# Scores of a banded attention in four 64x64 quarters of TensorE, with the two triangles merged per half block

## The chip, the cores and the metric

One core of one Trainium2 chip. The metric is the device time of one execution in microseconds, taken as the median of several runs. TensorE is called PE below, its weight loads PEld, VectorE DVE, ScalarE ACT, GpSimd POOL, and the queue of SyncE, which issues the transfers, SP.

## The reference

Attention over a band of 128 keys, with a linear bias, and a gated FFN on its output, all in fp32:

```python
B, H, S, D = 8, 8, 576, 64
scores = q @ k.T / sqrt(D)                      # per batch and head
rel = pos[:, None] - pos[None, :]
scores = where((rel >= 0) & (rel < 128), scores - slope[h] * abs(rel), -1e9)
attn = exp(scores - max); attn = attn / (sum(attn) + 1e-9)
x = (attn @ v), heads put side by side          # 4608 tokens x 512
out = (sigmoid(x @ w_gate) * (x @ w_val)) @ w_out   # 512 -> 1536 -> 512
```

## The kernel before

**Attention.** Two heads of a batch make a unit (32 units). Their 2 x 576 tokens are laid end to end and cut into 9 blocks of 128 queries, so that block 4 holds the end of one head and the start of the other. A block i needs the keys of blocks i-1 and i: in the band of 128, query row r sees key column c of its own block where c <= r, and key column c of the block before where c > r. So of the 256 scores of a row just 128 count, one in each column c, and the kernel merges the two triangles into one 128 x 128 tile.

The head size of 64 fills half of the rows of the array. The keys lie twice in SBUF, on partitions 0 to 63 and 64 to 127, and the queries of even and odd blocks on the one half or the other (`kraw`, `qraw`). The 288 blocks of all units form one stream. `scores` (L332) takes a call of 8 of them at a time, or of 4 for the first 72 blocks: block k of the call runs on row half r = k % 2 and is number a = k // 2 there. L346 multiplies 128 queries (weights) by 256 keys (128 for i = 0, which has no block before it) into half of a PSUM bank. There are four such banks, `sp` = mm2 to mm5, two for each row half; a bank holds two blocks. An fp32 matmul runs as two passes, each with its own weight load and its own row in the profile.

Then follow, in this order:

- L359, DVE: one copy_predicated per bank copies, where the mask `before` (L203, key column > row) is set, the score of the block before over that of the own block, for both blocks of the bank at once
- L367, DVE: per block, bias added, scaled, and the minimum (the negated maximum) of each row taken, from PSUM to the SBUF tile `pb`
- L370, ACT: exp, with the sum of each row
- L385, L387, DVE, for three blocks at once: 1 / sum; L390 on ACT or L391 on DVE: the product with it
- L395, PE: three blocks transposed; L178 on ACT (or L179 on DVE): copied to SBUF; L406, POOL: split into the two triangles again
- L432, PE: the value call, one per unit. It uses the array as two column halves of 64, one for each head of the unit, all 128 rows each, 13 matmuls with two passes. Its loop (L418 to L427) gives the columns that stream: for the first head 3 x 256 + 128 + 64 + 64 = 1024, for the second 192 + 256 + 256 + 192 + 64 + 64 + 64 = 1088.

**FFN.** A first pass over four of the twelve chunks of the hidden size (L474 gate and value, L513 output) runs beside the attention, on PE in every gap of it. Its weights are decoded early on ACT and DVE (L265 to L269, then L178, L179 and L187). A second pass over the other chunks (L605 and L513) follows.

**Order.** All operations go into one graph with a cost, a time at which they are wanted (`want`) and, for the attention, an earliest time (`release`). `Graph.order` simulates the engines with these costs and always picks the operation that can start first, among equals the one wanted first; FFN matmuls are wanted last. The result is the order in which each engine gets its instructions: engines work in that order and wait on semaphores. In the first 30 us `warm` (L232) fills gaps that the planner sees on PE with matmuls on the identity.

Of the kernel before, what the change touches and what calls it, by code (L numbers as in the profile page):

```python
# [9 lines left out]
I32 = mybir.dt.int32  # L10
F32R = mybir.dt.float32r
AF = mybir.ActivationFunctionType
ALU = mybir.AluOpType
PSUM = bass.MemoryType.PSUM

P = 128
B, H, S, D = 8, 8, 576, 64
# [14 lines left out]
RUN = 8  # L32
# [115 lines left out]
def dve_cost(n, psum=False, two=False):  # L148
    return 0.07 + n * (0.00104 if psum or two else 0.00053)
# [7 lines left out]
def attention_gated_ffn(ctx: ExitStack, tc: tile.TileContext, qd, kd, vd, wg, wv, wo, out):  # L157
    nc = tc.nc
    ctx.enter_context(tc.manual_schedule())
    g = Graph()  # L160
# [6 lines left out]
    att = att_ctx.enter_context(tc.tile_pool(name="att", bufs=1))  # L167
# [3 lines left out]
    def T(pool, name, shape, dtype, tag=None):  # L171
        if name not in made:
            made[name] = pool.tile(shape, dtype, tag=tag or name, name=name)
        return made[name]
# [22 lines left out]

    rel = moe.tile([P, 3, P], F32, tag="pi0", name="rel")
    nc.gpsimd.iota(rel[:, 0], [[-1, P]], base=0, channel_multiplier=1, allow_small_or_imprecise_dtypes=True)
    before = att.tile([P, 2, P], I32, name="before")  # L200
    nc.vector.tensor_scalar(rel[:, 1], rel[:, 0], 0.0, None, op0=ALU.is_lt)
    for a in range(2):
        nc.vector.tensor_copy(before[:, a], rel[:, 1])  # L203
    nc.vector.scalar_tensor_tensor(rel[:, 2], rel[:, 1], float(P), rel[:, 0], op0=ALU.mult, op1=ALU.add)
    relm = [att.tile([P, 5, P], F32, name=f"relm{p}") for p in range(NPAIR)]
    f = -8.0 * 2.0 ** -1
# [18 lines left out]
    mm = [ps_m.tile([P, NB], F32, name=f"mm{i}") for i in range(8)]  # L225
    sp = [t.rearrange("p (a q) -> p a q", a=2) for t in mm[2:6]]
# [80 lines left out]
    kraw = lambda u: T(att, f"kr{u.l}", [P, TOK], F32)  # L307
    qraw = lambda u: T(att, f"qr{u.l}", [P, (NBLK + 1) // 2, P], F32)
# [16 lines left out]
    def three_of(u, i):  # L325
        m = u.n * TRI + i // TRI
        e = i % TRI
        st = lambda: T(att, f"st{m % NST}", [P, 9], F32)
        pb = lambda: T(att, f"pb{m % NPB}", [P, TRI, P], F32)
        return m, e, st, pb, ("st", m % NST), ("pb", m % NPB)  # L330

    def scores(blks):  # L332

        u0, i0 = blks[0]
        want = u0.when(i0)
        slack = 0.0 if u0.n < HEAD else SLACK
        spot = [(k % 2, k // 2) for k in range(len(blks))]
        half = len(blks) == RUN // 2 and stages[0] % 2
        stages[0] += 1
        bank_of = lambda r, a: r * (RUN // 4) + a // 2 + half  # L340

        def matmuls():
            for (u, i), (r, a) in zip(blks, spot):
                lo = P if i == 0 else 0
                rows = slice(r * D, r * D + D)
                nc.tensor.matmul(sp[bank_of(r, a)][:, a % 2, lo:], qraw(u)[rows, i // 2],  # L346
                                 kraw(u)[rows, (i - 1) * P + lo:(i + 1) * P], start=True, stop=True)

        used = {}
        for (u, i), (r, a) in zip(blks, spot):  # L350
            used.setdefault(bank_of(r, a), []).append((u, i, a % 2))
        cost = sum(max(0.216 if i == 0 else 0.432 for (u, i), (r, b) in zip(blks, spot) if b == a) for a in {a for r, a in spot})
        g.add("PE", cost, matmuls, [("qr", u.l, i) for u, i in blks] + [("kr", u.l, j) for u, i in blks for j in (i - 1, i) if j >= 0],
              [("mm", 2 + b) for b in used], want, slack=slack, release=max(u.rel(i) for u, i in blks), mode=1)
        for b, on in sorted(used.items(), key=lambda kv: blks.index(kv[1][0][:2])):
            a = [a for u, i, a in on if i]
            if a:
                a0, a1 = a[0], a[-1] + 1
                g.add("DVE", dve_cost((a1 - a0) * P, psum=True), lambda b=b, a0=a0, a1=a1: nc.vector.copy_predicated(  # L359
                    sp[b][:, a0:a1, P:], before[:, a0:a1], sp[b][:, a0:a1, 0:P]), ["before"], [("mm", 2 + b)], want)  # L360
        for (u, i), (r, a) in zip(blks, spot):
            def one(u, i, b, a):
                m, e, st, pb, kst, kpb = three_of(u, i)
                want = u.when(i)
                mid = NBLK // 2
                w = 0 if i == 0 else 1 if i < mid else min(4, i - mid + 2)
                g.add("DVE", 0.21, lambda: nc.vector.tensor_tensor_reduce(  # L367
                    pb()[:, e], sp[b][:, a, P:], relm[u.p][:, w], op0=ALU.add, op1=ALU.min,
                    scale=-0.125, scalar=3.0e38, accum_out=st()[:, e:e + 1]), [("mm", 2 + b)], [(kpb, e), (kst, e)], want)
                g.add("ACT", 0.39, lambda: nc.scalar.activation(  # L370
                    pb()[:, e], pb()[:, e], AF.Exp, bias=st()[:, e:e + 1], scale=-1.0, accum_out=st()[:, 3 + e:4 + e]),
                    [(kst, e)], [(kpb, e), (kst, 3 + e)], want)
            one(u, i, bank_of(r, a), a % 2)
            if i % TRI == TRI - 1:
                probabilities(u, i - TRI + 1)
            if i == NBLK - 1:
                values(u)
# [282 lines left out]
    for u in units:  # L660
        if u.n + NSLOT - 1 < len(units):
            load(units[u.n + NSLOT - 1])
        while at < (u.n + 1) * NBLK:
            n = RUN // 2 if at < SOON * NBLK else RUN
            scores(stream[at:at + n])
            at += n
        if u.n == 0:
            todo = [(src, kind, i) for i0 in range(0, FC1, GRP) for src, kind in ((wg, "g"), (wv, "v")) for i in range(i0, i0 + GRP)]
            for k, (src, kind, i) in enumerate(todo + [(wo, "o", i) for i in range(FC1)]):
                prepare(w1, src, kind, i, W0 + WSTEP * k)  # L670
        if u.p == NPAIR - 1:
            while todo1 and (todo1[0] + 1) * NB <= (u.b + 1) * S:
                if todo1[0] >= LATE and banks[0] == 2:
                    banks[0] = 8
                    g.add("PY", 0.0, lambda: None, [], [TP, TAIL], FIRST)
                ffn(todo1.pop(0), w1)
# [11 lines left out]
    for f0 in range(FC1, NFC, FC1):  # L688
        w = Weights("w2", lambda: pools["w2"], list(range(f0, f0 + FC1)), ["w2pool"])
# [68 lines left out]
```

## Time and profile before

| | |
|---|---|
| median of 3 runs | 1048.82 us (1048.61 to 1049.87) |
| profiled execution: span, first to last instruction | 1047.7 us |
| busy: PE, PEld | 1036.2, 905.9 us |
| busy: DVE, ACT, POOL | 702.9, 518.1, 109.4 us |
| L346, scores on PE | 576 passes, 74.2 us |
| L359, merges on DVE | 144 |
| L432, values on PE | 832 passes, 67.4 us |

For the profiled execution the page gives the span; its time with what lies around the span is not listed, so sums are made against the span or, with the difference of 1.1 us left as it is, against the median.

In the groups, `64*128 64x256` is a weight tile of 64 rows by 128 columns and 64 partitions by 256 elements of the moving operand. A number after the bar is the time in which at least one instruction of the group ran, and after the comma the mean length of one in ns; instructions of one engine overlap, so count times mean can exceed the busy time. In a timeline, a row starts at its first number and lasts for its second. In rows of windows, the number in brackets counts instructions.

### The profile page before, as it was taken

The page shows a single profiled execution, that of the slowest core. Times are in us where ns is not written, and L with a number is a line of the kernel's source. Part 1 is how long each engine was busy: PE and PEld are TensorE (multiplying, and loading weights), DVE is VectorE, ACT ScalarE, POOL GpSimd, SP SyncE. Part 2 cuts the span into 40 slices and gives each one's busy share as a digit, 9 for nine tenths or more (in the row PEclk, how much of TensorE's full clock was granted, in tenths as well). Part 3 has the DMA queues.
Part 4 walks back from the last instruction along what each step waited for, and adds up shares of the span by engine and source line. Part 5 has one row for each costly group of instructions (what it writes and reads, how often), then busy time and mean ns, then how long its engine had stood idle before and what let it go on. Part 6 is the DMA issues. An engine that isn't in the chain of part 4 may idle for free.

```text
span 1047.7 us, 17053 instructions
## 1 busy us (share of the span) xinstructions
PE 1036.2 (99%) x5952; PEld 905.9 (86%) x5952; DVE 702.9 (67%) x1989; ACT 518.1 (49%) x1421; POOL 109.4 (10%) x202
## 2 busy tenths in 40 slices
PE   9999999999999999999999999999999999999998
PEld 7677777888887888888989999898999989899997
DVE  8989857565756249855757465666998566574643
ACT  6998757566755534432425243352744335242331
POOL 2423222222222210000000000000010000000000
PEclk9999999999999999999999999999999999999999
DMA  8767654554551315540241523324362241505112
GB/s 290 249 219 247 227 169 157 160 188 123 173 197 46 115 61 180 183 162 31 91 152 31 181 71 110 115 67 156 106 228 97 98 141 42 171 16 176 65 57 101
DMA packets 74726, 142.67 MB, mean 136 GB/s; under 512 B 7312, under 2 KB 30224, under 8 KB 74640
## 3 DMA queue, kind: packets, MB, share of 16 engines
q1 hardware_dynamic: 74640, 141.58, 41.1%
q8 instruction: 47, 0.77, 0.3%
q14 instruction: 39, 0.32, 0.1%
HBM read 103.81 MB, written 37.75 MB: 135 GB/s over the span
## 4 chain that ended last, share of the span: by engine, by line
PE 93%; DVE 3%; ACT 3%; DMA 0%; issue 0%; SPq 0%; ACTq 0%; DVEq 0%
PE mm L605 33%; PE mm L513 28%; PE mm L474 18%; PE mm L346 5%; PE mm L432 5%; PE mm L395 3%; ACT pb L370 1%; DVE wbits L269 1%; DVE mm L359 0%; DVE pb L367 0%; DMA kr<-in_k_dram 0%; PE mm L232 0%; ACT both L178 0%; ACT pb L390 0%; DVE pb L391 0%
## 5 line engine op out<-in xcount | busy, mean ns | idle before, releaser
L605 PE MATMUL mm<-xc,w2s 128*128 128x384 f32 x2016 | 354.4, 335 | 0.0
L605 PEld LDWEIGHTS mm<-xc,w2s 128*128 128x128 f32 x2016 | 351.3, 188 | 2.0
L513 PE MATMUL mm<-w2o,hh 128*128 128x512 f32 x576 | 177.7, 390 | 0.0
L406 POOL TENSOR_SCALAR_AFFINE_SELECT pt<-both 128x384 f32<-128x384 f32 x192 | 103.8, 564 | 268.9 <-ACT both L178 257.2
L513 PEld LDWEIGHTS mm<-w2o,hh 128*128 128x128 f32 x576 | 107.8, 188 | 21.2
L370 ACT ACTIVATE pb<-pb,st 128x128 f32<-128x128 f32 x288 | 112.7, 395 | 26.0 <-DVE st L367 25.8
L513 PE MATMUL mm<-w2o,hl 128*128 128x512 f32 x288 | 112.4, 390 | 0.0
L616 ACT ACTIVATE sg<-mm 128x384 f32<-128x384 f32 x96 | 47.2, 493 | 116.7 <-PE mm L605 77.7
L178 ACT COPY a<-mm 128x384 f32<-128x384 f32 x48 | 23.1, 482 | 151.8 <-PE mm L605 148.8
L513 PE MATMUL mm<-w1o,hh 128*128 128x512 f32 x288 | 92.2, 401 | 1.2 <-DVE hl L187 1.2
L474 PE MATMUL mm<-xhi,w1v 128*128 128x512 f32 x288 | 91.8, 400 | 1.0 <-ACT sg L485 1.0
L474 PE MATMUL mm<-xhi,w1g 128*128 128x512 f32 x288 | 92.4, 402 | 0.0
L612 DVE TENSOR_TENSOR mm<-mm,a 128x384 f32<-128x384 f32 x48 | 27.1, 564 | 74.7 <-PE mm L605 74.7
L359 DVE COPY_PREDICATED mm<-before,mm 128x256 f32<-128x256 int32 (+1 forms) x144 | 50.3, 394 | 37.3 <-PE mm L346 36.3
L346 PE MATMUL mm<-kr,qr 64*128 64x256 f32 (+1 forms) x576 | 74.2, 380 | 0.5 <-DMA kr<-in_k_dram 0.4
L432 PEld LDWEIGHTS mm<-pt,vr 128*64 128x64 f32 x832 | 61.2, 137 | 13.1 <-issue 9.0
L367 DVE CUSTOM_DVE_ANT_0 pb<-mm,relm 128x128 f32<-128x128 f32 x288 | 69.1, 283 | 3.0 <-PE mm L395 2.6
L432 PE MATMUL mm<-pt,vr 128*64 128x256 f32 (+2 forms) x832 | 67.4, 306 | 0.6 <-POOL pt L406 0.6
L178 ACT COPY both<-mm 128x384 f32<-128x384 f32 x95 | 45.1, 475 | 41.3 <-PE mm L395 32.7
L346 PEld LDWEIGHTS mm<-kr,qr 64*128 64x128 f32 x576 | 52.9, 186 | 13.5 <-issue 6.5
L513 PEld LDWEIGHTS mm<-w2o,hl 128*128 128x128 f32 x288 | 54.0, 188 | 11.3
L474 PEld LDWEIGHTS mm<-xhi,w1v 128*128 128x128 f32 x288 | 51.9, 188 | 13.0 <-issue 1.6
(101 smaller groups left out, 1496.8 us busy)
## 6 DMA issues: line engine op xcount, KB each, us to landing
part<-ob SPq DMA_DIRECT2D x72, 256.0 KB, 3.1
pi<-part SPq DMA_DIRECT2D x72, 256.0 KB, 3.3
kr<-in_k_dram SPq DMA_DIRECT2D x31, 576.0 KB, 4.4
xr<-xs SPq DMA_DIRECT2D x18, 768.0 KB, 4.8
qr<-in_q_dram SPq DMA_DIRECT2D x31, 320.0 KB, 4.9
vr<-in_v_dram SPq DMA_DIRECT2D x32, 288.0 KB, 3.1
xs<-xt SPq DMA_DIRECT2D x32, 288.0 KB, 2.9
out_dram<-ob SPq DMA_DIRECT2D x36, 256.0 KB, 2.2
```

What stands on the lines that cost most here:

```text
L178: g.add("ACT", act_cost(n, psum), lambda: nc.scalar.copy(out(), src()), reads, writes, want, release=release, ways=[("DVE", dve_cost(n, ps ...
L346: nc.tensor.matmul(sp[bank_of(r, a)][:, a % 2, lo:], qraw(u)[rows, i // 2], kraw(u)[rows, (i - 1) * P + lo:(i + 1) * P], start=True, stop= ...
L359: g.add("DVE", dve_cost((a1 - a0) * P, psum=True), lambda b=b, a0=a0, a1=a1: nc.vector.copy_predicated(sp[b][:, a0:a1, P:], before[:, a0:a ...
L367: g.add("DVE", 0.21, lambda: nc.vector.tensor_tensor_reduce(pb()[:, e], sp[b][:, a, P:], relm[u.p][:, w], op0=ALU.add, op1=ALU.min, scale= ...
L370: g.add("ACT", 0.39, lambda: nc.scalar.activation(pb()[:, e], pb()[:, e], AF.Exp, bias=st()[:, e:e + 1], scale=-1.0, accum_out=st()[:, 3 + ...
L395: nc.tensor.transpose(tp[:, e], pb()[:, e], ident)
L406: nc.gpsimd.affine_select(pt(u)[:, f0:f0 + 2 * n - 1:2, :], both(), [[0, n], step], cmp, 0.0, base=0, channel_multiplier=mult)
L432: nc.tensor.matmul(to()[e * D:(e + 1) * D, a - e * S - t0:b - e * S - t0], vraw(u)[:, c], seen, start=first, stop=last, skip_group_check=True)
L474: nc.tensor.matmul(mm[s], w.tile(kind, wi)[:, i, c * P:(c + 1) * P], x()[:, c, :], start=(k == 0 and c == 0), stop=(k == 2 and c == KC - 1))
L513: nc.tensor.matmul(mm[s], x()[:, i, ts], w.tile("o", wi)[:, i, :], start=(i == 0 and k == 0), stop=(i == n - 1 and k == 2))
L605: nc.tensor.matmul(mm[b][:, 0:N2], w.tile2(i, wp)[:, wk, c * P:(c + 1) * P], combo(k, xp)[:, c], start=(start and c == 0 and j == 0), stop ...
L616: g.add("ACT", act_cost(N2, psum=True), lambda: nc.scalar.activation(sg[h](), bk(b)(), AF.Tanh, scale=0.5), [("mm", b)], [("sg", h)], F)
```

## The change

A block is cut into two halves of 64 queries, h = 0 and 1. Half h goes to column half h of the array, so that a matmul uses one quarter, 64 rows by 64 columns, and the two halves of the two blocks on the row halves can be in the array at once. Half a block needs just 192 keys: h = 0 takes the 128 keys of the block before and the first 64 of its own, h = 1 the last 64 of the block before and all 128 of its own. In the PSUM slot of 256 columns, h = 0 stands at columns 64 to 255 and h = 1 at 0 to 191, so that after merging 64 columns both have their 128 scores at columns 64 to 191. For i = 0 the 192 columns come from two matmuls (128 and 64 keys) whose unneeded half is taken from keys that the bias masks.

The merge becomes two copy_predicated per bank, one for each half, on 64 partitions and 2 x 64 elements, with a mask `swap` that holds for h = 0 "own key at or before the row" and for h = 1 "key after the row". The planner's costs change with it: a call counts 0.16 us per block + 0.05 (it was 0.432 us for each pair), a merge `dve_cost(128)` twice for `dve_cost(256)`.

```diff
-    before = att.tile([P, 2, P], I32, name="before")
+    swap = att.tile([P, 2, D], I32, name="swap")
     nc.vector.tensor_scalar(rel[:, 1], rel[:, 0], 0.0, None, op0=ALU.is_lt)
     for a in range(2):
-        nc.vector.tensor_copy(before[:, a], rel[:, 1])
+        nc.vector.tensor_scalar(swap[0:D, a], rel[0:D, 0, 0:D], 0.0, None, op0=ALU.is_ge)
+        nc.vector.tensor_copy(swap[D:P, a], rel[D:P, 1, D:P])
...
-        bank_of = lambda r, a: r * (RUN // 4) + a // 2 + half
+        place = lambda r, a: r * (RUN // 2) + a + 2 * half
 
         def matmuls():
-            for (u, i), (r, a) in zip(blks, spot):
-                lo = P if i == 0 else 0
-                rows = slice(r * D, r * D + D)
-                nc.tensor.matmul(sp[bank_of(r, a)][:, a % 2, lo:], qraw(u)[rows, i // 2],
-                                 kraw(u)[rows, (i - 1) * P + lo:(i + 1) * P], start=True, stop=True)
+            for k in range(0, len(blks), 2):
+                for x, h in [(0, 0), (1, 1), (0, 1), (1, 0)]:
+                    for (u, i), (r, a) in [(blks[k + x], spot[k + x])]:
+                        j, row, col, k0 = place(r, a), slice(r * D, r * D + D), slice(h * D, h * D + D), i * P
+                        q = qraw(u)[row, i // 2, col]
+                        if i:
+                            jobs = [((1 - h) * D, k0 - P + h * D, 3 * D)]
+                        else:
+                            jobs = [(D, k0, P), (0 if h else 3 * D, k0 + h * D, D)]
+                        for c0, k1, n in jobs:
+                            nc.tensor.matmul(sp[j // 2][col, j % 2, c0:c0 + n], q, kraw(u)[row, k1:k1 + n], start=True, stop=True)
...
-        cost = sum(max(0.216 if i == 0 else 0.432 for (u, i), (r, b) in zip(blks, spot) if b == a) for a in {a for r, a in spot})
-        g.add("PE", cost, matmuls, [("qr", u.l, i) for u, i in blks] + [("kr", u.l, j) for u, i in blks for j in (i - 1, i) if j >= 0],
+        g.add("PE", 0.16 * len(blks) + 0.05, matmuls, [("qr", u.l, i) for u, i in blks] + [("kr", u.l, j) for u, i in blks for j in (i - 1, i) if j >= 0],
               [("mm", 2 + b) for b in used], want, slack=slack, release=max(u.rel(i) for u, i in blks), mode=1)
-                g.add("DVE", dve_cost((a1 - a0) * P, psum=True), lambda b=b, a0=a0, a1=a1: nc.vector.copy_predicated(
-                    sp[b][:, a0:a1, P:], before[:, a0:a1], sp[b][:, a0:a1, 0:P]), ["before"], [("mm", 2 + b)], want)
+        for b in used:
+            for h in range(2):
+                col, to, of = slice(h * D, h * D + D), D + h * D, 0 if h else 3 * D
+                g.add("DVE", dve_cost(2 * D, psum=True), lambda b=b, col=col, to=to, of=of: nc.vector.copy_predicated(
+                    sp[b][col, :, to:to + D], swap[col], sp[b][col, :, of:of + D]), ["before"], [("mm", 2 + b)], want)
...
-                    pb()[:, e], sp[b][:, a, P:], relm[u.p][:, w], op0=ALU.add, op1=ALU.min,
+                    pb()[:, e], sp[j // 2][:, j % 2, D:D + P], relm[u.p][:, w], op0=ALU.add, op1=ALU.min,
```

How this stands in the engines' orders: first PE, the score call of blocks 1 to 8 of unit 23 (mm2 to mm5 are the four banks, kr2 and qr2 its keys and queries), with its neighbours, before:

```order
L513 MATMUL mm1_144<-w1o0_1180,hl_921 128x512
L346 MATMUL mm2_145<-kr2_173,qr2_175 128x256
L346 MATMUL mm4_147<-kr2_173,qr2_175 128x256
L346 MATMUL mm2_145<-kr2_173,qr2_175 128x256
L346 MATMUL mm4_147<-kr2_173,qr2_175 128x256
L346 MATMUL mm3_146<-kr2_173,qr2_175 128x256
L346 MATMUL mm5_148<-kr2_173,qr2_175 128x256
L346 MATMUL mm3_146<-kr2_173,qr2_175 128x256
L346 MATMUL mm5_148<-kr2_173,qr2_175 128x256
L395 MATMUL mm6_149<-ident_71,pb6_341 128x128 x3
```

And the first half of the same call now, L354 being the line of its matmuls; eight more rows of the same kind follow on mm3 and mm5:

```order
L516 MATMUL mm0_145<-w1o0_1382,hl_1082 128x512
L354 MATMUL mm2_147<-kr2_175,qr2_177 64x192
L354 MATMUL mm4_149<-kr2_175,qr2_177 64x192
L354 MATMUL mm2_147<-kr2_175,qr2_177 64x192
L354 MATMUL mm4_149<-kr2_175,qr2_177 64x192
L354 MATMUL mm2_147<-kr2_175,qr2_177 64x192
L354 MATMUL mm4_149<-kr2_175,qr2_177 64x192
L354 MATMUL mm2_147<-kr2_175,qr2_177 64x192
L354 MATMUL mm4_149<-kr2_175,qr2_177 64x192
```

Each matmul of 256 columns has become two of 192, whose outputs lie on 64 partitions; the call stands between the same kinds of neighbours. In the whole of PE's order the warm-up matmuls behind the first score call are 45 in place of 40.

On DVE, the merges of two banks in unit 4 (pb and st are the tiles that the reductions write), before:

```order
L367 ISA pb5_300,st3_268<-mm5_148,relm0_83 128x128
L367 ISA st3_268 128x1
L359 COPY_PREDICATED mm2_145<-before_78,mm2_145 128x2x128
L359 COPY_PREDICATED mm4_147<-before_78,mm4_147 128x2x128
L367 ISA pb5_300,st3_268<-mm2_145,relm0_83 128x128
L367 ISA st3_268 128x1
```

And now:

```order
L370 ISA pb5_332,st3_297<-mm5_150,relm0_85 128x128
L370 ISA st3_297 128x1
L362 COPY_PREDICATED mm2_147<-swap_78,mm2_147 64x2x64
L362 COPY_PREDICATED mm4_149<-swap_78,mm4_149 64x2x64
L362 COPY_PREDICATED mm2_147<-swap_78,mm2_147 64x2x64
L362 COPY_PREDICATED mm4_149<-swap_78,mm4_149 64x2x64
L370 ISA pb5_332,st3_297<-mm2_147,relm0_85 128x128
L370 ISA st3_297 128x1
```

The place in the queue is the same, with four merges where there were two; over the whole kernel there are 288 in place of 144.

More of the change, by code (lines that the diff above doesn't have):

```diff
@@ L349, in scores @@
-        used = {}
-        for (u, i), (r, a) in zip(blks, spot):
-            used.setdefault(bank_of(r, a), []).append((u, i, a % 2))
-        cost = sum(max(0.216 if i == 0 else 0.432 for (u, i), (r, b) in zip(blks, spot) if b == a) for a in {a for r, a in spot})
-        g.add("PE", cost, matmuls, [("qr", u.l, i) for u, i in blks] + [("kr", u.l, j) for u, i in blks for j in (i - 1, i) if j >= 0],
-              [("mm", 2 + b) for b in used], want, slack=slack, release=max(u.rel(i) for u, i in blks), mode=1)
@@ L355, in scores @@
[L355 to L359, printed above, removed]
-                    sp[b][:, a0:a1, P:], before[:, a0:a1], sp[b][:, a0:a1, 0:P]), ["before"], [("mm", 2 + b)], want)
-        for (u, i), (r, a) in zip(blks, spot):
-            def one(u, i, b, a):
+            for k in range(0, len(blks), 2):
[9 more added lines that the diff above has]
+                            nc.tensor.matmul(sp[j // 2][col, j % 2, c0:c0 + n], q, kraw(u)[row, k1:k1 + n], start=True, stop=True)
@@ new lines, in scores @@
+        used = sorted({place(r, a) // 2 for r, a in spot}, key=lambda b: [place(r, a) // 2 for r, a in spot].index(b))
+        g.add("PE", 0.16 * len(blks) + 0.05, matmuls, [("qr", u.l, i) for u, i in blks] + [("kr", u.l, j) for u, i in blks for j in (i - 1, i) if j >= 0],
+              [("mm", 2 + b) for b in used], want, slack=slack, release=max(u.rel(i) for u, i in blks), mode=1)
+        for b in used:
[3 more added lines that the diff above has]
+                    sp[b][col, :, to:to + D], swap[col], sp[b][col, :, of:of + D]), ["before"], [("mm", 2 + b)], want)
@@ L363, in one @@
+        for (u, i), (r, a) in zip(blks, spot):
+            def one(u, i, j):
                 m, e, st, pb, kst, kpb = three_of(u, i)
@@ L367, in one @@
                 g.add("DVE", 0.21, lambda: nc.vector.tensor_tensor_reduce(
[L368 to L369 removed]
+                    pb()[:, e], sp[j // 2][:, j % 2, D:D + P], relm[u.p][:, w], op0=ALU.add, op1=ALU.min,
+                    scale=-0.125, scalar=3.0e38, accum_out=st()[:, e:e + 1]), [("mm", 2 + j // 2)], [(kpb, e), (kst, e)], want)
                 g.add("ACT", 0.39, lambda: nc.scalar.activation(
@@ L372, in one @@
                     [(kst, e)], [(kpb, e), (kst, 3 + e)], want)
-            one(u, i, bank_of(r, a), a % 2)
+            one(u, i, place(r, a))
             if i % TRI == TRI - 1:
```

## The prediction

> **What bounds the kernel now.** I read the page first: busy times, the 40 slices and the shares of the chain that ended last.
>
> ```profile
> span 1047.7 us, 17053 instructions
> PE 1036.2 (99%) x5952; PEld 905.9 (86%) x5952; DVE 702.9 (67%) x1989; ACT 518.1 (49%) x1421; POOL 109.4 (10%) x202
> ...
> PEclk9999999999999999999999999999999999999999
> ...
> PE 93%; DVE 3%; ACT 3%; DMA 0%; issue 0%; SPq 0%; ACTq 0%; DVEq 0%
> ```
>
> TensorE carries 93% of the chain at an unthrottled clock. The page's share is a mean over stages, so I cut the span with the busy times by window, before and after the moment (107.7 us) at which PE stops waiting:
>
> ```profile
> core 0: us, PE busy (x) PEld busy (x) DVE busy (x) ACT busy (x) POOL busy (x), PEclk, DMA share, GB/s
> 35.00:107.70 72.70, 68.27 (x486) 52.15 (x482) 66.82 (x287) 65.20 (x241) 26.85 (x42) 1.00 0.71 235
> 107.70:386.60 278.90, 278.71 (x1861) 225.51 (x1860) 165.84 (x810) 170.95 (x590) 69.67 (x135) 1.00 0.44 144
> ```
>
> Two regimes. Up to 107.7 us VectorE (66.82 of 72.70) and ScalarE are nearly full, since the decoding of the weights lies there beside the attention, and PE waits. From 107.7 to the end of the attention PE is busy 278.71 of 278.90 us and VectorE idles 113 us: a microsecond taken off PE there is a microsecond off the end. The scores, L346, split like this:
>
> ```profile
> core 0: us, PE busy (x) PEld busy (x), PEclk, DMA share, GB/s
> 0.00:107.60 107.60, 28.32 (x208) 18.95 (x208) 1.00 0.75 254
> 107.60:337.60 230.00, 45.76 (x368) 33.94 (x368) 1.00 0.49 160
> ```
>
> An fp32 matmul shows as two passes, so a score call of 8 blocks is 16 rows. 368 / 16 = 23 calls lie where PE is the bound; the 208 rows before are 104 blocks, namely 18 calls of 4 blocks and 4 of 8.
>
> **The score call on PE.** These are timeline rows of PE for one call of 4 blocks and one of 8, each with what follows it:
>
> ```profile
> 12.94 1.14 PE L346 MATMUL mm<-kr,qr 64*128 64x256 f32 x8
> 14.01 0.38 PE L232 MATMUL mm<-ident 128*128 128x128 f32 x1
> ...
> 183.29 1.99 PE L346 MATMUL mm<-kr,qr 64*128 64x256 f32 x16
> 185.21 2.08 PE L432 MATMUL mm<-pt,vr 128*64 128x256 f32 x26
> 187.22 0.33 PE L395 MATMUL mm<-ident,pb 128*128 128x128 f32 x1
> ```
>
> Start to start, 4 blocks take 14.01 - 12.94 = 1.07 us and 8 blocks 185.21 - 183.29 = 1.92. The two row halves run side by side, so a half streams 2 blocks x 2 passes x 256 = 1024 columns in the first and 2048 in the second: 0.85 / 1024 = 0.83 ns per column, and 0.22 us fixed (first weight load, emptying of the array). The value call L432 checks this on column halves: its longer half streams 1088 columns twice (the loop at L418 to L427), 2176 x 0.83 = 1.81, and it takes 187.22 - 185.21 = 2.01, so 0.20 fixed. In a row, its halves would need 4224 columns, 3.5 us; so column halves also run side by side.
>
> After the change each quarter of the array streams 8 x 192 = 1536 columns in a call of 8 blocks. If the four quarters run side by side, that is 1536 x 0.83 + 0.20 = 1.475 us, a saving of 0.445. I take the 0.20 of L432, whose weight loads are 64 columns wide as the new ones are. Bounds: 1.495 with the 0.22 of the old call, 1.44 if the shorter first load takes off a further 0.04 (the loads in the rows below differ by 186 - 137 = 0.049). A first block (i = 0) streamed 128 columns before, beside a partner with 256, and now streams 128 + 64 beside a partner with 192: nothing more. A call of 4 blocks: 768 x 0.83 + 0.20 = 0.84, a saving of 0.23.
>
> 23 calls x 0.445 = **10.2 us** where PE is the bound (9.8 to 11.0).
>
> No row of before splits rows and columns at once, so their running together is the step that could fail. What the two separate splits show: the weight loads hide.
>
> ```profile
> L432 PEld LDWEIGHTS mm<-pt,vr 128*64 128x64 f32 x832 | 61.2, 137 | 13.1 <-issue 9.0 <-POOL pt L406 3.0
> L346 PEld LDWEIGHTS mm<-kr,qr 64*128 64x128 f32 x576 | 52.9, 186 | 13.5 <-issue 6.5 <-DMA kr<-in_k_dram 0.8 <-DVE st L387 0.7
> ```
>
> The 26 loads of one value call sum to 3.6 us at 137 ns and its streams fill 1.8 of 2.01 us, so loads of one column half run beside streams of the other, although both use all rows. The new call has 32 passes in 1.475 us, 46 ns each, against 77 in L432 (26 in 2.01). That rate is not shown for a whole call.
>
> **The merges on VectorE.** Per bank, one copy_predicated of 128 x 256 becomes two of 64 x 128.
>
> ```profile
> L359 DVE COPY_PREDICATED mm<-before,mm 128x256 f32<-128x256 int32 x112 | 44.4, 424 | 33.5 <-PE mm L346 32.6
> L359 DVE COPY_PREDICATED mm<-before,mm 128x128 f32<-128x128 int32 x32 | 9.3, 290 | 3.8 <-PE mm L346 3.8
> ...
> 185.32 0.76 DVE L359 COPY_PREDICATED mm<-before,mm 128x256 f32<-128x256 int32 x2 [0.23 <-PE mm L346]
> ```
>
> Two in a row take 0.76, the last 0.43 of it by the mean above, so one follows the other after 0.33. A 128-wide one is 0.134 shorter (424 - 290), so 0.20; I take the same for 64 partitions, the duration going with the elements per partition. A full bank goes from 0.33 to 0.40 (+0.07), one with a first block from 0.20 to 0.40 (+0.20).
> - After 107.7 us: 92 banks, about 20 of them with a first block: 72 x 0.07 + 20 x 0.20 = 9 us. VectorE would then be busy 175 of 269 us. Its 94 idle us hide that, so nothing. The merge waits in VectorE's queue ahead of the reductions L367 and of whatever FFN work follows; the next score call, which needs the bank, comes some 10 us later (230 us / 23). If that cover went, the whole 9 us would be due.
> - Before 107.7 us: 52 banks, 12 with a first block: 40 x 0.07 + 12 x 0.20 = 5.2 us on an engine with 5.9 us of idle time left from 35 us on.
>
> **The early part.** What carries the chain there:
>
> ```profile
> by line: ACT pb L370 12.2%; PE mm L346 9.9%; PE mm L474 9.4%; PE mm L432 7.5%; DVE wbits L269 5.7%; DVE mm L359 4.8%; DVE pb L367 4.7%; DMA kr<-in_k_dram 4.1%; PE mm L395 4.1%; PE mm L513 3.2%; PE mm L232 3.1%; ACT both L178 3.1%; issue 2.9
> ```
>
> Of 107.7 us, 10.7 are scores. All early scores lose 18 x 0.23 + 4 x 0.445 = 5.9 of 28.3 us, 21%: -2.2 on the chain. Merges hold 5.2 us of the chain and grow by a third (52 x 0.40 against 40 x 0.33 + 12 x 0.20): +1.7. The planner fills PE's gaps with warm-up matmuls (L232) and, with shorter scores, places 45 of them after the first call where there were 40; fills hold 3.3 us of the chain, so +0.4. Sum -0.1; I take **0**. Bounds: -5.9 if all early score time was on the path, +6.4 if none was and all 5.2 of merges and 5 fills of 0.23 are. The four small operations that build the mask swap, in place of two, cost nothing: the first merge waits for PE,
>
> ```profile
> 5.79 0.29 DVE L359 COPY_PREDICATED mm<-before,mm 128x128 f32<-128x128 int32 x1 [0.17 <-PE mm L346]
> ...
> 6.19 1.64 PE L346 MATMUL mm<-kr,qr 64*128 64x256 f32 x10 [0.43 <-DMA kr<-in_k_dram]
> ```
>
> and the next score matmuls wait for keys from memory. After 386.6 us the change touches nothing: the FFN keeps its matmuls and its order, and starts earlier by what was saved. Where PE no longer stands in scores, the next thing late is PE again, with FFN matmuls.
>
> **Sum.** The profiled execution spans 1047.7 us; the median of the runs is 1048.82, so 1.1 us lie around the span, and I leave them. 1048.82 - 10.2 + 0 = **1038.6 us**.
>
> **Rivals.**
> - VectorE takes over early. If the part up to 107.7 us is bound by VectorE throughout, the merges' 5.2 us land whole and the early scores bring nothing: 1048.8 - 10.2 + 5.2 = 1043.8. For: 66.82 of 72.70 busy. Against: the chain there has scores on it twice as long as merges. The Trainium skill, "TensorEngine Tiling (Array Packing)", PSUM Bottleneck, warns that packing speeds up TensorE but not the emptying of PSUM, which may become the bottleneck; the row of 107.7 to 386.6 us speaks against that for the later part, the row before it for this rival.
> - Slower: weight loads cannot hide beside streams in the same rows. A row half now holds two column quarters. If each round (one pass of both) had to wait for its two loads, at 0.049 for 64 columns, 8 rounds add 0.78: 2.26 us per call, +0.34. 23 x 0.34 = 7.8, and early (18 x 0.16 + 4 x 0.34) x 10.7/28.3 = 1.6: 1058.2. It decides from 0.028 per load on, where the call is back at 1.92. Against: the value call, where this would give 1.81 + 26 x 0.049 = 3.1 instead of 2.01. For: nothing here mixes both splits. The Trainium skill, "TensorE: Matmul & The Clock Gate", Part 3 (The mechanism), says that a weight load overlaps matmuls in flight only when its row group differs; the two quarters of a row half share theirs, so by the page this rival would hold, and the value call's rows disagree with it.
> - Quarters run only two at a time: 3072 x 0.83 + 0.20 = 2.75 per call, +0.83; 23 x 0.83 = 19.1, early (18 x 0.40 + 4 x 0.83) x 0.38 = 4.0: 1071.9. The change would then not do what it says. Against: rows and columns each run in parallel now.
> - The gain is lost in the queues: the new order makes PE wait late for merges or transposes in most calls, by about the 0.445 us saved: 1048.8. Against: PE's idle time in that window is 0.2 us in all, with VectorE idle 41%.
>
> **Chances.** Forecast 0.72, VectorE early 0.12, loads 0.08, two at a time 0.03, lost in queues 0.05. About 0.2% (2 us) is what can be told from no change here: so faster 0.86 (the first two, and part of the last), same 0.03, slower 0.11. The range: 1034 (11.0 late and 4 of the early 5.9) to 1046 (9.8 late, +6.4 early, and a little of the queues) leaves out the slower cases and some tails, about 2 in 10.
>
> **What would show it.** Right: 8-block calls of about 1.47 us start to start in the chain; L346's successor with some 58 us busy in place of 74.1 (27 x 0.445 + 18 x 0.23 less); merges x288 at about 290 ns; PE full from about 107 us on; the attention over some 10 us or more earlier, the FFN part unchanged. Wrong: calls of 2 us and more (loads or pairs), or new PE waits on VectorE after 107 us, or a PE that becomes gapless 5 us later than before.

## The result and the profile after

| | before | after |
|---|---|---|
| median, same chip | 1048.92 us (1048.61 to 1049.87, 4 runs) | 1061.26 us (1059.43 to 1062.3, 4 runs) |
| span of the profiled execution | 1047.7 us | 1059.2 us |

The ratio is 1.0116, interval 1.0101 to 1.013: slower by 12.3 us, where 10.2 less were forecast. The page of the changed kernel: the busy times, two rows of the slices, and the chain.

```profile
span 1059.2 us, 18610 instructions
...
PE 1034.4 (98%) x6666; PEld 902.7 (85%) x6666; DVE 733.1 (69%) x2134; ACT 522.3 (49%) x1418; POOL 114.8 (11%) x206
...
DVE  8999977777676449754566575656999575674643
...
PEclk9899999999999999999999999999999999999999
...
PE 65%; DVE 1%; ACT 0%; issue 0%
```

TensorE is busy 1.8 us less than before in a span 11.5 us longer. It does its work, but waits more, and one slice of PEclk shows an 8. The groups of the two lines that the change touches:

```profile
L362 DVE COPY_PREDICATED mm<-swap,mm 64x128 f32<-64x128 int32 x288 | 73.8, 294 | 26.6 <-PE mm L354 22.2
L354 PE MATMUL mm<-kr,qr 64*64 64x192 f32 (+2 forms) x1280 | 63.1, 327 | 1.6 <-DVE st L370 1.2
```

The scores fell from 74.2 to 63.1 us of PE, where some 58 were forecast. The length of a merge, 294 ns, is nearly the 290 that was expected for it; what it costs is read from where the next one starts, below. Busy time by window, at the cuts of the prediction, and then the later part in three pieces:

```profile
core 0: us, PE busy (x) PEld busy (x) DVE busy (x) ACT busy (x) POOL busy (x), PEclk, DMA share, GB/s
35.00:107.70 72.70, 63.52 (x615) 47.51 (x613) 70.33 (x307) 63.19 (x233) 23.06 (x38) 0.95 0.63 210
107.70:386.60 278.90, 272.67 (x2324) 219.45 (x2323) 189.07 (x939) 174.61 (x603) 74.58 (x141) 0.99 0.47 156
...
107.70:140.00 32.30, 27.32 (x240) 19.85 (x241) 27.91 (x124) 21.42 (x76) 9.33 (x16) 0.95 0.63 217
140.00:165.00 25.00, 24.41 (x220) 19.51 (x211) 20.68 (x113) 17.35 (x66) 6.04 (x12) 1.00 0.62 204
165.00:386.00 221.00, 220.34 (x1870) 179.57 (x1871) 140.04 (x701) 135.84 (x461) 59.21 (x113) 1.00 0.43 143
```

From 35 to 107.7 us VectorE now works 70.33 of 72.70 us (it was 66.82) and PE 63.52 (68.27). VectorE stays at 27.91 of 32.30 until 140 us, and PE has next to no gaps only from about 165 us, where it had none from 107.7.

Two score calls of 8 blocks, in the timeline of PE, and the eight merges of one call, in that of VectorE, each with what follows:

```profile
239.47 1.59 PE L354 MATMUL mm<-kr,qr 64*64 64x192 f32 x36
240.99 0.73 PE L516 MATMUL mm<-w1o,hh 128*128 128x512 f32 x2
...
249.56 1.53 PE L354 MATMUL mm<-kr,qr 64*64 64x192 f32 x32
251.03 0.33 PE L398 MATMUL mm<-ident,pb 128*128 128x128 f32 x1
```

```profile
195.68 2.09 DVE L362 COPY_PREDICATED mm<-swap,mm 64x128 f32<-64x128 int32 x8 [0.28 <-PE mm L354]
197.80 0.29 DVE L370 CUSTOM_DVE_ANT_0 pb<-mm,relm 128x128 f32<-128x128 f32 x1
```

The first call takes 240.99 - 239.47 = 1.52 us with a first block in it (36 passes for 32), the second, without one, 251.03 - 249.56 = 1.47; 1.475 were forecast for both. The merges take 197.80 - 195.68 = 2.12 us, 0.265 each and **0.53 per bank**; 0.40 were forecast, and 0.33 is what the single merge had.

How far this set the attention back is seen at the value call of unit 8, first before, then after:

```profile
100.49 0.43 PE L432 MATMUL mm<-pt,vr 128*64 128x256 f32 x2
```

```profile
112.48 0.43 PE L435 MATMUL mm<-pt,vr 128*64 128x256 f32 x2
```

Up to these starts both had run the same 96 passes of the gate and value products and 9 of the output product. So after 8 units the changed kernel was **12.0 us** late, about as much as at the end: the gain forecast for the later part did not make it up. What ScalarE waited for between 8 and 160 us (total, times, longest), after and then before:

```profile
ACT pb L373 <- DVE st L370: 19.7, 21, 6.2
```

```profile
ACT pb L370 <- DVE st L367: 3.9, 5, 2.1
```

ScalarE's exp waited 19.7 us for VectorE's reductions, which stand behind the merges in VectorE's queue; before it was 3.9.

A second thing changed there. PE's granted clock, from windows of PE alone: first a gap and what follows it, then three more stretches at half clock, then the 3.41 us just ahead of each of the four, and the later part:

```profile
core 0: us, PE busy (x), PEclk, DMA share, GB/s
36.90:38.10 1.20, 0.00 (x1) 1.00 0.91 349
38.10:39.25 1.15, 0.91 (x3) 0.99 0.78 151
39.25:42.65 3.40, 3.03 (x28) 0.50 0.58 173
...
29.00:32.40 3.40, 3.38 (x33) 0.50 0.93 377
94.00:97.30 3.30, 3.30 (x9) 0.51 0.85 325
128.00:131.40 3.40, 3.40 (x38) 0.50 0.47 178
...
25.57:28.99 3.42, 1.94 (x31) 1.00 0.49 133
35.81:39.23 3.42, 1.84 (x27) 1.00 0.91 295
90.43:93.84 3.41, 2.07 (x17) 1.00 0.81 269
124.56:127.97 3.41, 1.48 (x5) 1.00 0.66 212
...
140.00:386.00 246.00, 244.75 (x2089) 1.00 0.45 149
```

PE stands still for 1.2 us, and about a microsecond after the gap its clock is at half for 3.4 us. There are four such stretches, all in the first 132 us, and each follows 3.41 us in which PE was busy for only 1.48 to 2.07; in the profile before, the clock was 1.00 throughout.

### The profile page after: what moved, and what is told of

Same layout as the page of the kernel before. It is cut to its first block, busy times and chain, and to the rows that moved or that the text cites. A ratio compares the mean times of both kernels' runs of the same rounds, so it can differ in the third digit from the quotient of the medians.

```text
span 1059.2 us, 18610 instructions
## 1 busy us (share of the span) xinstructions
PE 1034.4 (98%) x6666; PEld 902.7 (85%) x6666; DVE 733.1 (69%) x2134; ACT 522.3 (49%) x1418; POOL 114.8 (11%) x206
## 4 chain that ended last, share of the span: by engine, by line
PE 65%; DVE 1%; ACT 0%; issue 0%
PE mm L608 33%; PE mm L516 23%; PE mm L477 8%; PE mm L435 1%; DVE xlo L187 0%; PE mm L398 0%; DVE mm L493 0%; DVE hl L187 0%; DVE w2s L187 0%; DVE wbits L270 0%; DVE ob L521 0%; ACT sg L488 0%; ACT hh L178 0%; ACT wbits L266 0%; ACT xhi L178 0%
## 5 line engine op out<-in xcount | busy, mean ns | idle before, releaser
L362 DVE COPY_PREDICATED mm<-swap,mm 64x128 f32<-64x128 int32 x288 | 73.8, 294 | 26.6 <-PE mm L354 22.2
L435 PEld LDWEIGHTS mm<-pt,vr 128*64 128x64 f32 x832 | 61.9, 138 | 11.9 <-issue 8.9
L516 PEld LDWEIGHTS mm<-w1o,hh 128*128 128x128 f32 x288 | 51.8, 188 | 18.4 <-DVE w1o L187 3.8
L354 PE MATMUL mm<-kr,qr 64*64 64x192 f32 (+2 forms) x1280 | 63.1, 327 | 1.6 <-DVE st L370 1.2
L477 PEld LDWEIGHTS mm<-xhi,w1g 128*128 128x128 f32 x288 | 52.1, 191 | 14.2 <-DVE xhi L179 1.9
L521 DVE SCALAR_TENSOR_TENSOR ob<-mm,pi 128x512 f32<-128x512 f32 x72 | 48.2, 684 | 21.3 <-PE mm L516 12.5
```

The costliest lines, as they stand in the source:

```text
L354: nc.tensor.matmul(sp[j // 2][col, j % 2, c0:c0 + n], q, kraw(u)[row, k1:k1 + n], start=True, stop=True)
L362: g.add("DVE", dve_cost(2 * D, psum=True), lambda b=b, col=col, to=to, of=of: nc.vector.copy_predicated(sp[b][col, :, to:to + D], swap[col ...
L435: nc.tensor.matmul(to()[e * D:(e + 1) * D, a - e * S - t0:b - e * S - t0], vraw(u)[:, c], seen, start=first, stop=last, skip_group_check=True)
L477: nc.tensor.matmul(mm[s], w.tile(kind, wi)[:, i, c * P:(c + 1) * P], x()[:, c, :], start=(k == 0 and c == 0), stop=(k == 2 and c == KC - 1))
L516: nc.tensor.matmul(mm[s], x()[:, i, ts], w.tile("o", wi)[:, i, :], start=(i == 0 and k == 0), stop=(i == n - 1 and k == 2))
L521: g.add("DVE", dve_cost(DM, psum=True), lambda: nc.vector.scalar_tensor_tensor(ob(), mm[s], 0.5, pi(), op0=ALU.mult, op1=ALU.add), [("mm", ...
```

## The experiments

All ratios are to the kernel before on the same chip, with the 95% interval. "The order of before" means that every other instruction keeps the place that it has in the kernel before, on each engine.

### Parts of the change alone

**Quarters with the single merge.** Scores in quarters of 192 keys, written where before's layout wants them, merge as before, the change's cost for the planner:

```diff
+                for x, h in [(0, 0), (1, 1), (0, 1), (1, 0)]:
...
+                    c0, n = (h * D, 3 * D) if i else (P, P)
+                    nc.tensor.matmul(sp[bank_of(r, a)][col, a % 2, c0:c0 + n], qraw(u)[row, i // 2, col],
+                                     kraw(u)[row, (i - 1) * P + c0:(i - 1) * P + c0 + n], start=True, stop=True)
```

> The quarters of the change with the merge of before: half h = 0 streams keys into columns 0 to 191 of the old slot, h = 1 into columns 64 to 255, and one copy_predicated per bank on 128 partitions does the merge, as before the change. Theory A (the loss is VectorE time: two merges per bank take 0.53 us where one took 0.33, on an engine that is full up to about 125 us, so PE waits early): about 1038 us, PE gapless again from about 107 us, granted clock 1.000, score calls of 8 blocks at about 1.48 us. Rival B (the new order that the planner's smaller score cost makes is the bad one): 1055 to 1062, as the change. Rival C (quarter matmuls are short and let the TensorE clock drop): clock again near 0.994 with several throttled stretches before 130 us, 1050 or more.

Measured: 1045.64 against 1049.48, 0.9963 [0.9951, 0.9976]. Faster, but by 3.8 us only: something beside the merges costs.

**Two merges alone**, on before's scores; the other 64 columns of each half are left unmerged:

```diff
+            for h in range(2):
+                c0 = h * D
+                nc.vector.copy_predicated(sp[b][col, :, P + c0:P + c0 + D], before[col, :, c0:c0 + D], sp[b][col, :, c0:c0 + D])
```

> The scores of before (row halves, 256 keys) with two merges per bank of 64 partitions x 2 x 64 elements, one per half, in the same tile, as the change has them. It leaves out the merging of the other 64 columns of each half, whose values are then not those of the reference; the number and size of the operations are those of the change. Theory A: slower than the change's 1061, since the loss is there without the gain on PE: 1062 to 1070, VectorE idle for under 9 us in the first 110. B and C: near 1049, at most 1053.

Measured: 1065.84 against 1049.48, 1.0159 [1.0145, 1.0172]. Without the quarters' gain the two merges alone, placed by the planner, cost 16.4 us, more than the whole change.

**The planner's cost alone**: before, with `0.16 * len(blks) + 0.05` as the cost of a call.

> The kernel before with nothing changed but the planner's cost of a score call on PE (0.16 us per block + 0.05, as in the change). Theory A: 1046 to 1052, the order matters little. Rival B: 1055 or more, as the order alone would bring the loss. C: 1049.

Measured: 1055.66 against 1049.48, 1.0061 [1.0048, 1.0075]. The operations are those of before, but the planner does more than place them: where an operation can run on two engines it also picks the engine, so VectorE has 175 of the 288 products of L391 in place of 162, and PE has 88 warm-up passes in place of 80. What is called the effect of an order below has this in it. The windows show where PE lost the time:

```profile
85.00:100.00 15.00, 13.28 (x89) 10.39 (x89) 14.74 (x64) 13.22 (x49) 5.18 (x10) 1.00 0.85 296
100.00:116.00 16.00, 13.67 (x107) 11.22 (x108) 15.81 (x50) 11.91 (x45) 6.65 (x9) 0.89 0.58 198
116.00:130.00 14.00, 12.20 (x74) 9.25 (x73) 8.94 (x55) 9.82 (x39) 3.01 (x6) 0.88 0.78 246
```

VectorE is full (14.74 of 15, 15.81 of 16) while PE has gaps; the clock dips there as well.

**One of the two merges left out** (`for h in range(1)`): the change, with the triangles of every second half unmerged.

> The change without the merge of half h = 1 (left out, so the lower 64 rows of each block keep unmerged scores): one merge of 64 x 2 x 64 per bank, about 0.2 us. Theory A: VectorE has less to do than before the change, so 1031 to 1038 and clock 1.000. B: 1050 to 1058, as the order stays much as in the change. C: clock below 1.000 again and 1050 or more.

Measured: 1042.15, 0.9929 [0.9914, 0.9944]. With one merge per bank the change's own layout, mask and cost are faster than before. Two merges of the same half in VectorE's timeline, with what follows:

```profile
187.63 0.48 DVE L362 COPY_PREDICATED mm<-swap,mm 64x128 f32<-64x128 int32 x2 [0.17 <-PE mm L354]
188.03 0.28 DVE L370 CUSTOM_DVE_ANT_0 pb<-mm,relm 128x128 f32<-128x128 f32 x1
```

188.03 - 187.63 = 0.40 for two, 0.20 each: the price that the prediction took for all.

**The planner told the true price**, 0.13 us more for the second merge (`+ 0.13 * h`):

> The change with the planner told what a bank's second merge really takes (0.13 us more). A2: the work on VectorE is the same and it is full, 1058 to 1063. Rival G (the order is bad because the planner counts on merges that are too cheap): 1050 to 1056.

Measured: 1055.13, 1.0054 [1.0039, 1.0069]: 6 us better than the change, still slower than before.

### The planner's cost, separated

**Quarters and single merge, the old cost.** As the first experiment, with the cost of before.

> Quarters with the merge of before, and the planner's old score cost, so that every engine has the order of before and only the score matmuls differ. Theory A2 (three terms that add: quarters -10 on PE where it is the bound, the order that the smaller score cost makes +6, two merges per bank +16): 1036 to 1040, no throttled stretch of the clock beside the end. Rival D (quarters lose part of their gain whatever the order, by waits or the clock): 1043 to 1047, as the run with one merge and the new cost.

Measured: **1037.28** against 1049.17, 0.9884 [0.987, 0.9899]. This beats both kernels, and leaves nothing out. The orders of all engines are those of before, so it is the change in the scores alone: -11.9 us. The same two windows:

```profile
35.00:107.70 72.70, 65.89 (x629) 50.38 (x631) 66.94 (x285) 65.63 (x240) 27.12 (x42) 1.00 0.72 234
107.70:386.60 278.90, 278.70 (x2258) 226.67 (x2251) 173.82 (x823) 174.24 (x596) 70.47 (x135) 1.00 0.47 155
```

VectorE, ScalarE and PE stand as before (66.82, 65.20 and 68.27 early, PE 278.71 late). Its value calls of units 8 and 31:

```profile
98.93 0.43 PE L436 MATMUL mm<-pt,vr 128*64 128x256 f32 x2
...
364.74 0.43 PE L436 MATMUL mm<-pt,vr 128*64 128x256 f32 x2
```

They start 1.6 and 11.9 us earlier than before's (100.49 and 376.62): 1.6 gained early, 10.3 later.

**The change with the old cost:**

> The change with the planner's old score cost; nothing left out. A2: the order's 6 us come back, about 1055. Rival E (with two merges VectorE is full so long that the order no longer matters): 1059 to 1063.

Measured: 1057.79, 1.0084 [1.0069, 1.0099]: 3.5 us better than the change.

**Other costs in the 1037.28 kernel**, 0.19 and 0.14 per block in place of 0.16, both + 0.05:

> Quarters with the merge of before, and a score cost in the planner of 0.19 us per block + 0.05, between the old one (0.216) and the new (0.16). Theory H (a score counted too cheap lets the planner place too much beside it, and the loss grows steadily as the cost falls): about 1040, between 1037 and 1045. Rival I (any change of a cost deals a new order, better or worse by some us without a trend): not ordered by the cost, anywhere from 1035 to 1048.

> The same with 0.14 us per block + 0.05. H: 1047 to 1050, above the 1045.6 of 0.16. I: without a trend, anywhere from 1035 to 1048.

Measured: 1043.15 (0.9939 [0.9923, 0.9956]) and 1040.77 (0.9923 [0.9908, 0.9938]). With 0.16 it was 1045.64. So the time does not follow the number in one direction; each number gives another order, and these four orders lie within 8.4 us.

### The price of a merge

**All first halves, then all second halves** (the loops over banks and halves exchanged):

> The change with the merges of half h = 0 of all banks of a call ahead of those of h = 1, so that in calls of 8 blocks the wait of a bank's second merge for its first has three others in between. Theory A2 with the self-wait as part of the merges' price: the third merge of a group follows the one before after about 0.21 us in place of 0.31 in calls of 8, VectorE is busy some 5 us less, and the time falls by 1 to 4 us, to 1057 to 1060 (the early calls of 4 blocks have two banks, and keep the wait). Rival F (the 0.31 is not a wait for the own write but the cost of such an instruction): spacing unchanged, 1061.

Measured: 1056.08, 1.0068 [1.0051, 1.0086], with the planner free to place the merges. That is 5.2 us below the change and just below the 1057 to 1060 expected. Two calls with their eight merges in a row:

```profile
175.22 1.83 DVE L362 COPY_PREDICATED mm<-swap,mm 64x128 f32<-64x128 int32 x8
177.08 0.29 DVE L370 CUSTOM_DVE_ANT_0 pb<-mm,relm 128x128 f32<-128x128 f32 x1
...
184.82 2.08 DVE L362 COPY_PREDICATED mm<-swap,mm 64x128 f32<-64x128 int32 x8 [0.60 <-PE mm L354]
```

The first takes 177.08 - 175.22 = 1.86 us, 0.23 for each merge, where the change has 2.12; the second is as long as in the change. Over the whole kernel the merges keep VectorE busy for 69.6 us in place of 73.8. So halves in a row save VectorE some 4 us; what that is worth in time this run can't tell, since its order is a new one.

**The order of before, two merges per bank.** To take the planner out, both merges of a bank are issued by one step of its order, with the costs of before:

```diff
+            def both_halves(b=b):
+                for h in range(2):
+                    nc.vector.copy_predicated(sp[b][col, :, to:to + D], swap[col], sp[b][col, :, of:of + D])
+            g.add("DVE", dve_cost(n * P, psum=True), both_halves, ["before"], [("mm", 2 + b)], want)
```

> The change's quarters and its two merges per bank, but every engine in the order of before: the two merges of a bank stand where its one merge stood, one right behind the other, and the planner counts what it counted before. So the second waits each time for the first, and a bank should take about 0.65 us of VectorE in place of 0.33 (0.20 with a first block). Theory A2, merges alone without any new order: early 40 x 0.32 + 12 x 0.45 = 18 us more on VectorE, of which some 4 find idle time: 1049 to 1056, against 1037.3 with one merge. Rival J (the merges' share seen so far was mostly the luck of new orders): 1038 to 1044.

Measured: 1068.62 against 1049.06, 1.018 [1.0167, 1.0194].

```profile
194.78 2.60 DVE L364 COPY_PREDICATED mm<-swap,mm 64x128 f32<-64x128 int32 x8 [0.60 <-PE mm L354]
197.41 0.29 DVE L373 CUSTOM_DVE_ANT_0 pb<-mm,relm 128x128 f32<-128x128 f32 x1
```

197.41 - 194.78 = 2.63 us: every merge takes 0.33 and a bank 0.66, twice the single merge. In this kernel the halves change at every merge; in the change the planner put two of the same half together. Its value calls of units 8 and 31:

```profile
117.53 0.43 PE L438 MATMUL mm<-pt,vr 128*64 128x256 f32 x2
...
394.29 0.43 PE L438 MATMUL mm<-pt,vr 128*64 128x256 f32 x2
```

17.0 and 17.7 us later than before's: nothing of the quarters' late gain is left, and PE waits late too, after 165 us, where it was busy for 220.34 us in the change:

```profile
165.00:386.00 221.00, 216.90 (x1858) 174.76 (x1851) 150.57 (x731) 136.49 (x483) 58.04 (x112) 1.00 0.45 148
```

**The order of before, one merge per block** of 128 partitions and 128 columns, in the 1037.28 kernel:

> Quarters in the old layout, every engine in the order of before, and the merge of a bank as two of 128 x 128, one for each block, one right behind the other; a bank with a first block keeps its single one. Theory A2: early 40 x 0.32 = 13 us more on VectorE, some 4 of it in idle time: 1043 to 1048. J: 1037 to 1041.

Measured: 1042.9, 0.9939 [0.9926, 0.9953].

```profile
196.58 1.87 DVE L365 COPY_PREDICATED mm<-before,mm 128x128 f32<-128x128 int32 x7
198.36 0.28 DVE L373 CUSTOM_DVE_ANT_0 pb<-mm,relm 128x128 f32<-128x128 f32 x1
```

198.36 - 196.58 = 1.78 for seven, 0.25 each, although the partitions never change. Two causes were possible for a merge that takes 0.33 in place of 0.20: it waits for the write that the merge just before it made in the same bank, or the half of the partitions changes. The next two runs separate them.

**The first half merged twice** (`for h in (0, 0)`): the wait stays, the partitions don't change; the second half is left unmerged.

> Same order and operations as the kernel with two merges in the order of before (1068.6 us, eight merges in 2.63 us), but both merges of a bank are those of the first half, so the partitions never change between merges; the second half's triangles are left unmerged. Theory W (a merge drains the engine because it waits for the write just before it in the same bank): each second merge still waits, so 0.32 + 0.20 per bank, eight merges in about 2.1 us; the time falls to about 1043, like the run with one merge per block, which had 0.53 per bank. Theory S (it drains because the half of the partitions changes): nothing changes, so 0.20 per merge, eight merges in 1.64 us, and about 1040. If neither is right and two merges of 64 partitions simply cost 0.33 each, 2.6 us and 1068 again.

**One merge per bank, of the first half in banks 0 and 1, of the second in 2 and 3** (`for h in (b // 2,)`): the partitions change each time, no merge follows one in its own bank; half of the merging is left out.

> As before, but one merge of 64 partitions per bank, of the first half in banks 0 and 1 and of the second half in banks 2 and 3, which follow each other in turn, so every merge changes the half of the partitions and none waits for the write just before it; the other half of each bank is left unmerged. Theory S (change of the half): 0.31 to 0.34 per merge, four merges in about 1.28 us, as the one merge of 128 partitions has, so about 1037 to 1038. Theory W (wait for the own write): 0.20 per merge, four in 0.82 us, and the early part gains some 4 us on that: about 1034.

Measured: 1049.41 against 1049.35, 1.0001 [0.9991, 1.001], and 1042.15, 0.993 [0.9916, 0.9945]. The merges of a call, first of the one, then of the other:

```profile
201.01 2.16 DVE L364 COPY_PREDICATED mm<-swap,mm 64x128 f32<-64x128 int32 x8
203.09 0.28 DVE L373 CUSTOM_DVE_ANT_0 pb<-mm,relm 128x128 f32<-128x128 f32 x1
```

```profile
195.85 1.27 DVE L364 COPY_PREDICATED mm<-swap,mm 64x128 f32<-64x128 int32 x4
197.15 0.29 DVE L373 CUSTOM_DVE_ANT_0 pb<-mm,relm 128x128 f32<-128x128 f32 x1
```

With the wait alone, eight take 2.08 us: at 0.20 for the four that follow another bank's, the four that wait take 0.32. With the change of partitions alone, four take 1.30, 0.325 each. So each of the two lengthens a merge by itself, and both together (0.33 in the order of before) are no worse than one. In the second run this holds for the last merge too, which is one of a second half and is followed by a reduction on all 128 partitions: at 0.20 for it the four would take some 1.2 us. After a first half that reduction follows in 0.20 (the run with one of the two merges left out). Both halves of the question were answered with yes; neither expectation had that. The times were missed upwards: 1049.41 where 1043 or 1040 was expected, 1042.15 where 1037 or 1034 was.

**What else is in the 1042.15.** A bank's merge takes 0.33 there as in the 1037.28 kernel, in the same order, and yet it is 4.9 us slower. Two things of the change were added to the 1037.28 kernel: a second matmul of 64 keys for each half of a first block (its output unused), and then merges of both blocks also where one is a first block.

```diff
-                    for c0, k1, n in [(c0, (i - 1) * P + c0, n)]:
+                    for c0, k1, n in [(c0, (i - 1) * P + c0, n)] + [(h * D, h * D, D)] * (not i):
...
-                    sp[b][:, a0:a1, P:], before[:, a0:a1], sp[b][:, a0:a1, 0:P])
+                    sp[b][:, :, P:], before, sp[b][:, :, 0:P])
```

> The kernel with quarters, one merge and the order of before (1037.28 us), with one thing of the change added: each half of a first block takes a second matmul of 64 keys, as in the change, its output unused. The run with halves by bank (1042.15 us) differs from 1037.28 by this and by merges of the full width in banks with a first block. Theory M (the added matmuls cost): about 1040 to 1041. Theory V (the wider merges cost, on VectorE): 1037.3 to 1038.

> As before, and the one merge of 128 partitions takes both blocks of its bank also where one of them is a first block, as in the change. 11 early banks then cost 0.13 us more each, 1.4 us of VectorE in the part that it bounds, and 20 later ones where it has time. Theory M: 1 to 1.5 us above the kernel with the added matmuls alone, so about 1042. Theory V: about 1041 to 1042, all of it from this step. Both: this kernel ends near the 1042.15 of the run with halves by bank, whose merges also cost 0.33 per bank.

Measured: 1038.58 (0.99 [0.9885, 0.9915]) with the first, 1039.56 (0.9907 [0.9891, 0.9924]) with both. The first lies between what the two theories expected, the second below both. The medians step by 1.3 and 1.0 us; the intervals of neighbours overlap, so each step is near what can be told, and both together are 2.3. The first step fits the calls on PE: 20 of the 23 late ones hold a first block, and at 0.05 us each (1.52 against 1.47 in the change) that makes 1.0. The other 2.6 to 1042.15 stay open.

## Why the prediction was wrong

**The ladder.** All kernels but the last two have the order of before. Each row adds to the one above it. The kernels ran on several chips, on which the medians of before lie between 1048.9 and 1049.4.

| kernel | median | step | value call of unit 8, against before |
|---|---|---|---|
| before | 1048.9 | | |
| quarters, single merge | 1037.3 | -11.9 against its own chip's before | -1.6 |
| + first blocks split, merges at full width | 1039.6 | +2.3 | +0.1 |
| + half merges by bank in the change's layout, the partitions change | 1042.15 | +2.6 | +2.1 |
| + a second merge, 0.52 per bank | 1049.4 | +7.3 | +6.2 |
| + at 0.66 per bank | 1068.6 | +19.2 | +17.0 |
| the planner places both merges itself, old cost | 1057.8 | -10.8 | |
| the change: new cost | 1061.3 | +3.5 | +12.0 |

**The score call: right.** Quarters run side by side: 1.47 us without a first block, 1.52 with one, for 1.475; the 0.05 of a first block had been put at nothing. With the single merge and the order of before the scores keep PE busy for 57.6 us, as the 58 forecast; the 63.1 of the change hold 124 more passes (1280 for 1156) and stretches at half clock. In the order of before they save 10.3 us from unit 8 on, for the 10.2 of 23 calls. The early part gained 1.6 where the working had 2.2 on the chain. The rival that loads cannot hide beside streams of the same rows (2.26 us per call) and the one of two quarters at a time (2.75) fell. On loads, the Trainium skill, "TensorE: Matmul & The Clock Gate", Part 3 (The mechanism), says that a load overlaps matmuls in flight only when its row group differs, though it also speaks of a background weight buffer into which a load may go early. Two quarters here share their rows, and the 1.52 us disagree with the strict rule.

**The merges: the step that failed.** "I take the same for 64 partitions" and "A full bank goes from 0.33 to 0.40" took the 0.20 us by which one merge follows another of the same kind, and gave it to merges that follow one of another kind. 0.20 holds between merges of the same half in different banks. Where the half changes, or the merge before wrote the same bank, it is 0.32 to 0.33, as long as for twice the elements. So the change has 0.53 per bank. By the prediction's own sum, 52 early banks then cost 40 x (0.53 - 0.33) + 12 x (0.53 - 0.20) = 12.0 us on VectorE, not 5.2, against 5.9 us of its idle time.

**"The early part ... I take 0": failed for that reason.** The rival "VectorE takes over early" had the mechanism: VectorE went from 66.82 to 70.33 of 72.70 us, and the lateness at unit 8 is 12.0 us. It was given 0.12 and a price of 5.2. With 12.0 it would have read 1048.8 - 10.2 + 12.0 = 1050.6, slower and not faster. Its price decided the sign, but not the whole size: 10.7 us to the measured 1061.3 are left. The Trainium skill, "TensorEngine Tiling (Array Packing)", PSUM Bottleneck, warns that packing may make the emptying of PSUM the limit. Here the faster scores alone did not do that (VectorE 66.94 of 72.70 us with the single merge, 66.82 before); the doubled merges did (70.33).

**"PE full from about 107 us on": failed.** PE now waits until some 165 us. In the 57 us from 107.7 it idles for 4.98 + 0.59 = 5.6 us, where before it idled for 0.2 in the whole 278.90. After that the forecast held: PE is busy 220.34 of 221.00 us with merges at 0.53 per bank. At 0.66 it did not: 216.90 of 221.00.

**The difference, added up.** PE idles for 1059.2 - 1034.4 = 24.8 us of its span, before for 1047.7 - 1036.2 = 11.5: 13.3 more, and 5.6 of them are the ones above. Its work became only 1.8 us shorter, though the scores gave 11.1 (74.2 to 63.1): the warm-up grew by 1.8 (11.5 to 13.3 us, 90 passes for 80), and the half clock lengthens what runs at it, by at most the 6.8 us below. 13.3 - 1.8 are the 11.5 us by which the span grew.

**What was not priced.** That a new cost number gives another order, and other engines for some operations: +6.2 us by itself on before, +8.4 on the quarters with one merge, +3.5 on the change. The order had been looked at in two places, where it had not changed in kind.

**Open.** How much of the loss is the clock. Four stretches of some 3.4 us at half clock cost at most 4 x 3.4 x 0.5 = 6.8 us of PE. They follow gaps on PE. In the ten executions with the first half merged twice, the mean clock goes from 0.996 to 1.000 and the times don't follow it: 1049.17 us at 0.996, 1049.17 to 1050.11 at 1.000. With two merges in the order of before they do, 1066.36 us at 0.994 and 1068.88 at 0.990, and which of the two brings the other is not shown. Open is also why one order of the planner is better than another by up to 8 us.

## What to carry to other kernels

When one instruction is split in two, take its price from the same pair in the same sequence: the gap from start to start between instructions that alternate as the new ones will, not the length of one nor the gap in a row of like ones. Where an engine has 5.9 us left in the stage in question, a price that is off by 0.13 us on fifty instructions turns the sign, so look at both ends of it there before the mean over the kernel. And keep the old cost in a planner, or the old order, when measuring an edit: here a new order, with its choice of engines, was worth up to 8 us, which hid that the quarters by themselves gain 11.9.

## What the runs showed of the hardware

- VectorE's copy_predicated of 64 x 128 follows the one before after 0.20 us when both work on the same half of the partitions and in different banks, after 0.325 when the half changes (a reduction on all 128 partitions behind a merge of the second half waits as long), and after 0.32 when it waits for a write of the merge before it; 0.33 with both.
- Four 64 x 64 quarters in fp32 ran a call of 32 passes, 1536 columns each, in 1.47 us, where two row halves needed 1.92 for 2048.
- The granted clock halved for 3.4 us at a time in a stage where PE had gaps of about a microsecond, each time behind 3.41 us with PE busy for 1.48 to 2.07, and stayed at 1.00 where PE was busy 244.75 of 246.00 us. Gaps like these don't always bring it about: in the profile with the first half merged twice PE was busy 62.03 of 72.70 us, less than in the change, and from 38.31 us on for 1.69 of 3.41, at a clock of 1.00. Six of the ten executions of that kernel have a mean clock of 0.996 to 0.998. The row of the profile:

```profile
35.00:107.70 72.70, 62.03 (x618) 46.92 (x620) 70.34 (x309) 63.90 (x232) 24.71 (x41) 1.00 0.66 212
```
